# Linear attention followed by two expert stages: TensorE work of the attention grouped by tile shape, state in two buffers, state product in the rotating banks, powers of w in PSUM

## The chip, the cores and the metric

One core of one Trainium2 chip. The metric is the device time of one execution in microseconds (us), the median of several runs of the same program. Engines by the profile's names: PE (TensorE) and PEld (its weight loads), DVE (VectorE), ACT (ScalarE), POOL (GpSimd), SP (the queue that issues most DMAs). Each engine works through its own list of instructions in order; between engines there are semaphores.

## The reference

Three stages; the change touches only the first. All of it is fp32.

```
def _attn_ref(r, k, v, w, u):               # r, k, v: (4, 8, 768, 48)
    for t in range(S):
        cur = einsum('bhd,bhe->bhde', u * k[t], v[t])
        y[t] = einsum('bhd,bhde->bhe', r[t], state + cur)
        state = w * state + einsum('bhd,bhe->bhde', k[t], v[t])
x = attn_out as (3072, 384)
x = top-1 of 8 experts, softmax gate, relu(x @ w1[e]) @ w2[e]
out = g(x @ w_in) @ w_out,  g(h) = h - tanh(h)
```

## The kernel before

The 768 tokens of each of the 4 batches are cut into 6 chunks of 128. A step n is one chunk of one batch: `seq = [(c, b) ...]`, chunks outer, batches inner, so 24 steps (NN = 24) and a last half step that only finishes. The 8 heads lie as 4 pairs j with a half q each: partitions 64q to 64q+47 hold head 2j+q, and the pad up to 64 is zero. Per step:

- `load(n)` (L230) brings r, k, v by token (`n_b`, 576 KB) and r, k by dimension (`t_b`, two transfers of 192 KB), five buffers each, issued by SP three steps ahead. `w_load` (L66) brings 384 KB of the first expert's weights in every second step up to n = 15; `w_split` (L79) cuts them into a rounded part (ACT, L84) and a rest (DVE, L85).
- POOL makes `rk` (L317), `rku` (L323) and `kh` (L332), 128x384 each, two steps ahead, and `sw` (L376), the decayed state.
- DVE sums `rku` over each head into `dt` (`diag_sum`, L337), multiplies `t` by the powers of w in PRK (`scale`, L312, 1024 columns), and copies the scores below the diagonal into `am` (`mask`, L359, one instruction per half). `am` comes from ACT, eight diagonal tiles per step (`diag`, L344).
- PE makes the scores A (`scores`, L353, 64-row tiles), the state product Pp (`state`, L370, tiles of 48 columns), the output from the state (`outp`, L393, full 128x128 tiles against Sb, a block-diagonal copy of the state) and the output within the chunk (L398, 48 columns), and transposes finished outputs of seven steps ago (`xout`, L524). fp32 matmuls show as two instructions each.
- ACT copies the output Yp to SBUF (L403), the state into the block diagonal (`state_copy`, L385) and the transposed rows to `xs` (L531), which go to DRAM.
- Once in four steps the chunk just finished is gated: `logits` (L413, at n mod 4 = 1), `logits2` and `gate` (n mod 4 = 2, on PE, DVE, ACT), `rank_mm` and `rank_sel` (n mod 4 = 3: DVE up to `lo` and `ol`, then `hv` L490 and `rh` on POOL), `idx_mm` (n mod 4 = 0).

The order of each engine's list is the order of the calls in the loop at L702 (`manual_schedule`); nothing reorders it. PSUM has eight banks: yh0 and yh1 hold Yp, yh2 holds Pp, A0 and A1 the scores, sm the small products, and two banks with the tag X are taken in turn by Xps, lps and others: the third taker waits for the readers of the first.

```
        st["S", b] = n                  # end of state(n): Sc[b] = sw + Pp, in place
        ...
            if 1 <= n <= NN:
                outp(n - 1)             # L712, before scores(n)
                if n > 1:
                    state_copy(n - 1)
```

Of the kernel before, what the change touches and what calls it, by code (L numbers as in the profile page):

```python
# [8 lines left out]
F32 = mybir.dt.float32  # L9
# [6 lines left out]
ALU = mybir.AluOpType  # L16
# [14 lines left out]
def rwkv_moe_moe_kernel(ctx: ExitStack, tc: tile.TileContext, rk_t, rkv, pk, u, wp1, wp2, out):  # L31
# [141 lines left out]
    def bc(ap, shape):  # L173
        return ap.to_broadcast(shape)
# [27 lines left out]
    Sc = [ap_.tile([P, HP, D], F32, name=f"Sc{b}") for b in range(B)]  # L202
    Sb = [ap_.tile([P, HP, P], F32, name=f"Sb{b}") for b in range(B)]
# [3 lines left out]
    PRK = ap_.tile([P, 2, HP, P], F32, name="PRK")  # L207
# [5 lines left out]
    yh = [psy.tile([P, BANK], F32, tag=f"y{d}", name=f"yh{d}")[:, 0:HEAD] for d in range(KD)]  # L213
    Yp = [t.rearrange("p (j t) -> p j t", t=P) for t in yh[0:2]]
    Pb = yh[2]
    Pp = Pb[:, 0:HP * D].rearrange("p (j d) -> p j d", d=D)
# [52 lines left out]
    def tables():  # L269

        for t, base, n in ((pw, wsafe.unsqueeze(2), 16), (pq, pw[:, :, 16:17], 8)):
            nc.vector.memset(t[:, :, 0:1], 1.0)
            nc.vector.tensor_copy(out=t[:, :, 1:2], in_=base)
            m = 1
            while m < n:
                nc.vector.tensor_tensor(out=t[:, :, m + 1:2 * m + 1], in0=t[:, :, 1:m + 1],
                                        in1=bc(t[:, :, m:m + 1], [P, HP, m]), op=ALU.mult)
                m *= 2
        table(nc.gpsimd, PRK[:, 0], pq[:, :, 0:8], pw[:, :, 0:16])
        nc.vector.reciprocal(out=ipw, in_=pw)  # L280
        nc.vector.reciprocal(out=ipq, in_=pq)
        nc.vector.tensor_tensor(out=ipl, in0=ipq, in1=bc(pq[:, :, 8:9], [P, HP, 9]), op=ALU.mult)
        table(nc.vector, PRK[:, 1], ipq[:, :, 0:8], ipw[:, :, 1:17])

# [78 lines left out]
    def state(n):  # L363
        c, b = seq[n]
        if c == C - 1:
            return
        kh = st.pop(("kh", n))
        for j in range(HP):
            for q in range(2):
                nc.tensor.matmul(Pp[64 * q:64 * q + D, j, :], lhsT=kh[:, 2 * j + q, :],  # L370
                                 rhs=n_b[n % NB][:, 2, 2 * j + q, :], start=True, stop=True)
        if c == 0:
            nc.vector.tensor_copy(out=Sc[b], in_=Pp)
        else:
            sw = at2.tile([P, HP, D], F32, tag="sw", name="sw")
            nc.gpsimd.tensor_tensor(out=sw, in0=Sc[b], in1=bc(pq[:, :, 8:9], [P, HP, D]), op=ALU.mult)  # L376
            nc.vector.tensor_tensor(out=Sc[b], in0=sw, in1=Pp, op=ALU.add)
        st["S", b] = n

    def state_copy(n):  # L380
        c, b = seq[n]
        if c == C - 1:
            return
        for q in range(2):
            nc.scalar.copy(out=Sb[b][64 * q:64 * q + 64, :, 64 * q:64 * q + D], in_=Sc[b][64 * q:64 * q + 64, :, :])  # L385

    def outp(n):
        c, b = seq[n]
        am = st.pop(("am", n))
        for j0 in range(0, HP, 2):  # L390
            for j in (j0, j0 + 1):
                if c > 0:
                    nc.tensor.matmul(Yp[j % 2][:, j // 2, :], lhsT=Sb[b][:, j, :], rhs=t_b[n % NB][:, 0, j, :],  # L393
                                     start=True, stop=False)
            for j in (j0, j0 + 1):
                for q in range(2):
                    p0 = 64 * q
                    nc.tensor.matmul(Yp[j % 2][p0:p0 + D, j // 2, :], lhsT=n_b[n % NB][:, 2, 2 * j + q, :],  # L398
                                     rhs=am[:, q, j, :], start=(c == 0), stop=True)
        if b == 0:  # L400
            st["y", c] = yp.tile([P, HP, B, P], F32, tag="y", name="y")
        for i in range(2):
            nc.scalar.copy(out=st["y", c].rearrange("p (j i) b t -> p i j b t", i=2)[:, i, :, b, :], in_=Yp[i])  # L403

    sm = ps1.tile([P, 512], F32, tag="sm", name="sm")
# [203 lines left out]
    def by_token():  # L609

        with tc.tile_pool(name="slow", bufs=1) as sp:
# [3 lines left out]
            for b in range(B):  # L615
                nc.vector.memset(Sc[b], 0.0)
# [5 lines left out]
            for c in range(C):  # L622
                st["y", c] = yp.tile([P, HP, B, P], F32, tag="y", name="y")
                for b in range(B):
# [5 lines left out]
                    with tc.For_i(0, P, 1) as t:  # L630
# [8 lines left out]
                        nc.vector.tensor_add(out=cur, in0=cur, in1=Sc[b])  # L639
# [7 lines left out]
                        nc.vector.tensor_tensor(out=Sc[b], in0=Sc[b], in1=bc(wcol.unsqueeze(2), [P, HP, D]), op=ALU.mult)  # L647
                        nc.vector.tensor_add(out=Sc[b], in0=Sc[b], in1=kv)
# [12 lines left out]
    with tc.manual_schedule():  # L661
        w_cols()
        identity()
        for i in range(2):
# [8 lines left out]
        zero_states()  # L673
# [23 lines left out]
        for t in Yp + [Pp]:  # L697
            nc.vector.memset(t, 0.0)
# [3 lines left out]
        for n in range(NN + 1):  # L702
            if n + 3 < NN:
                load(n + 3)
            if n % 2 == 1 and n // 4 < PRE:
                w_load(n // 4, n // 2 % 2)
            if n + 1 < NN:
                diag_sum(n + 1)
                scale(n + 1)
            at_step(n, 2, logits)  # L710
            if 1 <= n <= NN:
                outp(n - 1)  # L712
                if n > 1:
                    state_copy(n - 1)
            for m in XOUT.get(n, (n - LAG,)):
                if m >= 0:
                    xout(m)
            if 0 < n < NN - 1:
                diag(n + 1)
            if n < NN:  # L720
                scores(n)
                mask(n)
                if n == 0:
                    k_table()
                    diag(1)
                else:
                    if n == 1:
                        state(0)
                    state(n)
            if n == 1:  # L730
                state_copy(0)
            if n + 2 < NN:
                side(n + 2)
                if n == 0:
                    side_kh(0)
                    side_kh(1)
                side_kh(n + 2)
# [8 lines left out]
            if n < NN:  # L746
                at_step(n, 5, idx_mm)
            if n == NN - 2:
                head_gather()
# [651 lines left out]
```

## Time and profile before

| what | us |
|---|---|
| median of 3 runs | 825.17 (825.07 to 829.99) |
| the profiled execution | 828.9 |
| its span, first to last instruction | 826.8 |
| PE busy | 786.1 (95%) |
| DVE busy | 649.6 (79%) |
| ACT busy | 526.5 (64%) |
| POOL busy | 448.3 (54%) |

The profiled execution is one run; its time is the span and 2.1 us around it. Times in rows count from the start of the span. Busy shares are means over all three stages; the attention is the stretch up to about 154 us, after which the expert stages follow on the same core.

### The profile page before, as it was taken

To read this page: it belongs to the slowest core of one execution; us is meant where nothing else is said; L and a number is where in the kernel's file an instruction comes from. 1 tells how busy PE (TensorE), PEld (TensorE's weight loads), DVE (VectorE), ACT (ScalarE), POOL (GpSimd) and SP (SyncE) were. 2 spreads that over 40 slices of the span, in tenths; PEclk is the share of its full clock that TensorE was granted. 3 is DMA by queue.
4 is the path that set the end of the run, shared out by engine and by line. 5 is a ranking of instruction groups with operands and counts; after the bars stand their busy time and mean duration, and the time that the engine had idled before them with its cause. 6 is when DMAs were issued, how large, how long until landed. Compare 5 with 4: busy or idle time off the path is not lost.

```text
span 826.8 us, 14401 instructions
## 1 busy us (share of the span) xinstructions
PE 786.1 (95%) x5052; PEld 702.3 (85%) x5052; DVE 649.6 (79%) x1127; ACT 526.5 (64%) x1135; POOL 448.3 (54%) x438
## 2 busy tenths in 40 slices
PE   7799999989999999997999999999999999999995
PEld 6576766789888999996989999999999999999895
DVE  6789888548888888876469888888888888888991
ACT  7778887515454444443478776776777677677870
POOL 5977876226675886656525535335344344443533
PEclk9799999999999999999999999999999999999999
DMA  8988774226688989897410000000000000000000
GB/s 202 246 222 238 220 211 129 99 71 201 201 227 236 256 224 267 258 250 177 110 56 2 1 1 39 1 1 39 1 1 29 10 1 17 23 1 0 39 1 38
DMA packets 34979, 89.88 MB, mean 109 GB/s; under 512 B 5690, under 2 KB 13022, under 8 KB 34896
## 3 DMA queue, kind: packets, MB, share of 16 engines
q1 hardware_dynamic: 30704, 78.87, 34.5%
q0 software_dynamic: 4192, 9.99, 3.9%
q8 instruction: 42, 0.69, 0.4%
q14 instruction: 41, 0.34, 0.2%
HBM read 73.10 MB, written 15.74 MB: 107 GB/s over the span
## 4 chain that ended last, share of the span: by engine, by line
PE 48%; DVE 2%; issue 1%; POOL 1%; ACT 0%; POOLq 0%; DVEq 0%; ACTq 0%
PE h L1237 23%; PE o L1285 22%; PE y L1011 2%; PE hps L986 1%; DVE t L1258 0%; DVE h L1255 0%; DVE h L1256 0%; DVE h L1254 0%; DVE t L1253 0%; POOL out_dram L1298 0%; POOL g L1274 0%; ACT g L1273 0%; POOLq L1396 0%; ACT z L1241 0%; ACT t L1243 0%
## 5 line engine op out<-in xcount | busy, mean ns | idle before, releaser
L1237 PE MATMUL h<-xb,ring 128*128 128x512 f32 x864 | 215.9, 395 | 0.7 <-DVE t L1258 0.7
L1274 POOL TENSOR_TENSOR g<-t,g 128x512 fp32r<-128x512 f32 x93 | 120.5, 1295 | 176.3 <-ACT g L1273 121.3
L1285 PE MATMUL o<-ring,g 128*128 128x384 f32 x1116 | 209.3, 336 | 0.0
L1285 PEld LDWEIGHTS o<-ring,g 128*128 128x128 f32 x1116 | 196.1, 188 | 8.1
L1237 PEld LDWEIGHTS h<-xb,ring 128*128 128x128 f32 x864 | 161.3, 188 | 31.9 <-DVE t L1258 1.1
L85 POOL TENSOR_TENSOR ring<-stg,ring 128x384 fp32r<-128x384 f32 x102 | 104.9, 1057 | 39.6 <-ACT ring L84 23.9
L1241 ACT ACTIVATE z<-h 128x512 f32<-128x512 f32 x96 | 57.5, 599 | 97.9 <-PE h L1237 97.8
L1011 PE MATMUL y<-h,ring 128*128 128x256 f32 (+7 forms) x576 | 115.5, 345 | 0.0
L986 PE MATMUL hps<-xt,ring 128*128 128x472 f32 (+6 forms) x504 | 106.8, 355 | 8.4 <-DVE xt L975 4.1
L1011 PEld LDWEIGHTS y<-h,ring 128*128 128x128 f32 x576 | 102.6, 190 | 3.5 <-DVE h L990 0.4
L986 PEld LDWEIGHTS hps<-xt,ring 128*128 128x128 f32 x504 | 90.7, 188 | 13.7 <-DVE xt L975 5.5
L1253 DVE TENSOR_TENSOR t<-t,h 128x512 f32<-128x512 f32 x96 | 65.8, 686 | 43.0 <-ACT t L1243 42.9
L84 ACT CAST ring<-stg 128x384 fp32r<-128x384 f32 x152 | 71.1, 511 | 29.3 <-DMA stg<-in_wp_dram 24.9
L1258 DVE COPY_PREDICATED t<-mk,h 128x512 f32<-128x512 uint32 x96 | 72.2, 752 | 9.9
L1255 DVE SCALAR_TENSOR_TENSOR h<-s,h 128x512 f32<-128x512 f32 x96 | 66.9, 696 | 10.0
L1245 ACT ACTIVATE s<-z,gb 128x512 f32<-128x512 f32 x96 | 69.6, 725 | 0.0
L1256 DVE SCALAR_TENSOR_TENSOR h<-z,h 128x512 f32<-128x512 f32 x96 | 66.8, 695 | 3.3
L1247 ACT ACTIVATE mk<-z,gt 128x512 f32<-128x512 f32 x96 | 69.3, 722 | 0.0
L989 ACT ACTIVATE h<-hps 128x256 fp32r<-128x256 f32 (+7 forms) x64 | 32.0, 501 | 57.7 <-PE hps L986 55.3
L1254 DVE TENSOR_TENSOR h<-h,z 128x512 f32<-128x512 f32 x96 | 66.5, 693 | 0.0
L344 ACT ACTIVATE am<-ident,dt 128x128 f32<-128x128 f32 x192 | 58.6, 389 | 7.0 <-DVE dt L337 6.9
L1273 ACT CAST g<-t 128x512 fp32r<-128x512 f32 x93 | 57.6, 619 | 8.0 <-DVE t L1258 5.8
(233 smaller groups left out, 1116.2 us busy)
## 6 DMA issues: line engine op xcount, KB each, us to landing
stg<-in_wp_dram SPq DMA_DIRECT2D x64, 384.0 KB
n<-in_rkv_dram SPq DMA_DIRECT2D x24, 576.0 KB
d<-in_wp_dram SPq DMA_DIRECT2D x32, 384.0 KB
t<-in_rk_t_dram SPq DMA_DIRECT2D x48, 192.0 KB
wdec<-dcf SPq DMA_DIRECT2D x32, 192.0 KB
xd<-xs SPq DMA_DIRECT2D x24, 192.0 KB
stg<-wdec SPq DMA_DIRECT2D x12, 384.0 KB
wl<-wdec SPq DMA_DIRECT2D x2, 768.0 KB
```

What stands on the lines that cost most here:

```text
L84: nc.scalar.copy(out=dst[:, 0, sl], in_=of)
L85: eng.tensor_tensor(out=dst[:, 1, sl], in0=of, in1=dst[:, 0, sl].bitcast(F32), op=ALU.subtract)
L986: nc.tensor.matmul(ps, lhsT=wf(a, kk), rhs=xt[e][b][:, kk, :], start=(n == 0), stop=(n == 8))
L1011: nc.tensor.matmul(yps[d], lhsT=wf(a)[:, d * P:(d + 1) * P], rhs=h2[:, b, :], start=(f == 0 and n == 0), stop=(f == CH1 - 1 and n == 2))
L1237: nc.tensor.matmul(ps, lhsT=wf(a, kk), rhs=xb[j][:, b, kk, :], start=(n == 0), stop=(n == 8))
L1245: nc.scalar.activation(out=s, in_=z, func=ACTF.Square, scale=G_K ** 0.5, bias=gb)
L1247: nc.scalar.activation(out=mk, in_=z, func=ACTF.Relu, scale=-1.0, bias=gt2)
L1255: nc.vector.scalar_tensor_tensor(out=ps, in0=s, scalar=G_K * G_D, in1=ps, op0=ALU.add, op1=ALU.mult)
L1256: nc.vector.scalar_tensor_tensor(out=ps, in0=z, scalar=G_A, in1=ps, op0=ALU.subtract, op1=ALU.mult)
L1258: nc.vector.copy_predicated(out=t, mask=mk.bitcast(U32), data=ps)
L1274: nc.gpsimd.tensor_tensor(out=g[:, 1, :], in0=ww, in1=g[:, 0, :].bitcast(F32), op=ALU.subtract)
L1285: nc.tensor.matmul(ops[q], lhsT=gg[i][:, b, q * P:(q + 1) * P], rhs=wf(a), start=(f == 0 and n == 0), stop=(f == CH2 - 1 and n == 2))
```

## The change

1. `outp` no longer uses the block-diagonal Sb: the output from the state is 8 matmuls with lhsT of 64 rows and 48 columns straight from the state `Sc`, which now has two buffers per batch (chunk parity). All 8 come first, then all 8 within the chunk, into one bank Yp. `state_copy` and `zero_states` go. So that rows 48 to 63 of the state are zero, `kh` gets 64 columns (three fixed buffers, pads zeroed once) and the state product writes 64 rows.
2. The state product Pp takes one of the two X banks instead of yh2. The powers of w (PR, PK) lie in the banks yh1 and yh2 that this leaves free, both made by DVE; `scale` becomes two instructions of 512 columns.
3. `y_copy` is one copy of 512 columns, called two steps later.
4. The order within a step: scores, mask, scale(n+1), xout, logits2 and gate, rank, idx, logits, state, output of step n-1, and POOL's side work last. Before: scale(n+1), logits, output of n-1, state copy, xout, diag, scores, mask, state, side work, logits2 and gate, rank, idx.

```diff
-        table(nc.gpsimd, PRK[:, 0], pq[:, :, 0:8], pw[:, :, 0:16])
+        table(nc.vector, PR, pq[:, :, 0:8], pw[:, :, 0:16])
...
-        nc.vector.tensor_tensor(out=t, in0=t, in1=PRK, op=ALU.mult)
+        for i, pw_ in enumerate((PR, PK)):
+            nc.vector.tensor_tensor(out=t[:, i], in0=t[:, i], in1=pw_, op=ALU.mult)
...
+        Pp = ps1.tile([P, HP, P], F32, tag="X", name="Pp", bufs=2)[:, :, 0:D]
...
-                nc.tensor.matmul(Pp[64 * q:64 * q + D, j, :], lhsT=kh[:, 2 * j + q, :],
+                nc.tensor.matmul(Pp[64 * q:64 * q + 64, j, :], lhsT=kh[:, 2 * j + q, :],
...
-                    nc.tensor.matmul(Yp[j % 2][:, j // 2, :], lhsT=Sb[b][:, j, :], rhs=t_b[n % NB][:, 0, j, :],
-                                     start=True, stop=False)
...
+                    nc.tensor.matmul(Yp[p0:p0 + D, j, :], lhsT=Sc[b][(c - 1) % 2][p0:p0 + 64, j, :],
+                                     rhs=t_b[n % NB][p0:p0 + 64, 0, j, :], start=(j == 0), stop=False)
...
             if n + 1 < NN:
                 diag_sum(n + 1)
-                scale(n + 1)
-            at_step(n, 2, logits)
-            if 1 <= n <= NN:
-                outp(n - 1)
...
+            at_step(n, 2, logits)
+            if 0 < n < NN:
+                if n == 1:
+                    state(0)
+                state(n)
+            if n > 0:
+                outp(n - 1)
```

POOL's list around step 15, before: `hv` and `rh` of the rank stand behind the side work of step 15 (the first `sw`, `rk`, `rku`, `kh` here).

```order
L376 TENSOR_TENSOR sw<-Sc_143,pq 128x192 [waits DVE_49]
L317 TENSOR_TENSOR rk<-n_132 128x384 [waits DMAHW4_49]
L323 TENSOR_TENSOR rku<-rk,ub 128x384 [waits DVE_49,Pool_49]
L332 TENSOR_TENSOR kh<-n_132,KT 128x384 [waits PE_49]
L490 TENSOR_TENSOR hv<-OH,ohh 128x128 [waits DVE_49,Activation_49]
L494 TENSOR_TENSOR rh<-hv,tileid 128x4x32 [waits Pool_49]
```

The same four and the same pair in the changed kernel:

```order
L487 TENSOR_TENSOR hv<-OH,ohh 128x128 [waits DVE_49,Activation_49]
L491 TENSOR_TENSOR rh<-hv,tileid 128x4x32 [waits Pool_49]
L376 TENSOR_TENSOR sw<-Sc_146,pq 128x192
L315 TENSOR_TENSOR rk<-n_132 128x384 [waits DMAHW4_49]
L321 TENSOR_TENSOR rku<-rk,ub 128x384 [waits Pool_49]
L330 TENSOR_TENSOR kh_158<-n_132,KT 128x8x48 [waits PE_49]
```

`hv` has moved ahead of the `sw` of step 15 and of the `rk` and `rku` of step 17; what it waits for on DVE is the same.

PE's list in step 17 (the one with the logits), before: logits, then the two halves of the output, the transposes, the scores, and the state product into its own bank yh_159.

```order
L413 MATMUL lps<-y,wgp 32x512 [waits Activation_49] x2
L413 MATMUL lps<-y,wgp 32x512 x2
L393 MATMUL yh_157<-t_126,Sb_144 128x128
...
L524 MATMUL Xps<-ident,y 128x128 x3
L353 MATMUL A_1706<-t_127 128x128 [waits DMAHW5_49,PE_49]
...
L370 MATMUL yh_159<-n_132,kh 48x48 [waits DMAHW4_49,DVE_49]
```

The same step in the changed kernel, from the transposes on; the row of Pp is the first state matmul, yh_159 is now Yp, L387 is the output from the state and L392 the output within the chunk.

```order
L521 MATMUL Xps<-ident,y 128x128 [waits Activation_49]
L521 MATMUL Xps<-ident,y 128x128 x3
L410 MATMUL lps<-y,wgp 32x512 [waits DVE_49,Activation_49]
L410 MATMUL lps<-y,wgp 32x512 x3
L369 MATMUL Pp<-n_132,kh_158 64x48 [waits DMAHW4_49,Activation_49,Pool_49]
L369 MATMUL Pp<-n_132,kh_158 64x48 x7
L387 MATMUL yh_159<-t_126,Sc_141 48x128 x8
L392 MATMUL yh_159<-am,n_131 48x128 x8
L351 MATMUL A_1768<-t_128 128x128 [waits DMAHW1_49,DVE_49]
```

The output now stands behind the state product, and the state product waits for ACT: in this step Xps and lps have taken both X banks, so Pp takes the bank of Xps of the same step, whose reader is `xs`.

## Rows read from the trace of the kernel before

**Rows 1.** Windows: busy of PE, PEld, DVE, ACT, POOL (count), PEclk, DMA share, GB/s.

```profile
30.00:40.00 10.00, 7.30 (x92) 5.94 (x86) 6.68 (x11) 6.95 (x23) 9.77 (x10) 0.72 1.02 247
100.00:120.00 20.00, 18.18 (x229) 13.12 (x223) 16.82 (x35) 15.29 (x47) 14.45 (x16) 1.00 0.78 219
```

**Rows 2.** Timeline of PE, scores of steps 4 and 20: start, length, instruction.

```profile
37.37 2.08 PE L353 MATMUL A<-t 64*128 64x128 f32 x16
...
132.77 1.16 PE L353 MATMUL A<-t 64*128 64x128 f32 x16
```

**Rows 3.** Timeline of PE, step 13, from its scores to its last transposes.

```profile
91.49 1.16 PE L353 MATMUL A<-t 64*128 64x128 f32 x16
92.58 0.56 PE L370 MATMUL yh<-n,kh 128*48 128x48 f32 x16
93.08 0.71 PE L393 MATMUL yh<-t,Sb 128*128 128x128 f32 x4
93.72 1.01 PE L398 MATMUL yh<-am,n 128*48 128x128 f32 x8
...
95.30 0.65 PE L398 MATMUL yh<-am,n 128*48 128x128 f32 x8
95.88 0.66 PE L524 MATMUL Xps<-ident,y 128*128 128x128 f32 x4
```

**Rows 4.** Timeline of DVE, steps 15 and 16, and the gate of step 22.

```profile
103.38 0.54 DVE L337 TENSOR_REDUCE dt<-rku 128x8 f32<-128x384 f32 x1
103.85 1.21 DVE L312 TENSOR_TENSOR t<-t,PRK 128x1024 f32<-128x1024 f32 x1
104.98 1.32 DVE L359 COPY_PREDICATED am<-mlt,A 128x512 f32<-128x512 uint32 x2
106.20 0.34 DVE L377 TENSOR_TENSOR Sc<-sw,yh 128x192 f32<-128x192 f32 x1
106.45 0.18 DVE L476 TENSOR_TENSOR pr<-sm,OH 128x32 f32<-128x32 f32 x1
...
107.59 0.69 DVE L501 TENSOR_TENSOR ol<-iotaf,lo 128x512 f16<-128x512 f32 x1
...
110.35 1.56 DVE L312 TENSOR_TENSOR t<-t,PRK 128x1024 f32<-128x1024 f32 x1
...
146.16 0.18 DVE L428 TENSOR_REDUCE m<-sm 128x4 f32<-128x32 f32 x1
...
147.85 0.16 DVE L451 TENSOR_TENSOR cums<-cum,bump 128x8 f16<-128x8 f16 x1
```

**Rows 5.** Timeline of POOL, side work and rank of steps 14 to 16.

```profile
99.43 1.00 POOL L317 TENSOR_TENSOR rk<-n 128x384 f32<-128x384 f32 x1
100.51 1.00 POOL L323 TENSOR_TENSOR rku<-rk,ub 128x384 f32<-128x384 f32 x1
...
107.63 0.92 POOL L490 TENSOR_TENSOR hv<-OH,ohh 128x128 f16<-128x128 f16 x1 [5.16 <-DVE lo L488]
...
109.45 1.38 POOL L317 TENSOR_TENSOR rk<-n 128x384 f32<-128x384 f32 x1
110.91 1.87 POOL L323 TENSOR_TENSOR rku<-rk,ub 128x384 f32<-128x384 f32 x1
```

**Rows 6.** Timeline of ACT, step 16: transposed rows, then the diagonals.

```profile
110.55 0.58 ACT L531 ACTIVATE xs<-Xps,gt 128x384 f32<-128x384 f32 x1
111.03 2.44 ACT L344 ACTIVATE am<-ident,dt 128x128 f32<-128x128 f32 x8
```

**Rows 7.** One line's instructions: DVE with one operand in PSUM (min/median/max ns).

```profile
L1253 DVE TENSOR_TENSOR t<-t,h x96: 657/688/691, 418.7 to 805.0; 128x512 f32<-128x512 f32 x96
```

**Rows 8.** Timeline around step 3: DVE's sum and PE's output.

```profile
32.19 0.55 DVE L337 TENSOR_REDUCE dt<-rku 128x8 f32<-128x384 f32 x1 [2.51 <-POOL rku L323]
...
34.98 2.46 PE L398 MATMUL yh<-am,n 128*48 128x128 f32 x16 [2.70 <-DVE am L359]
```

**Rows 9.** Timeline of PE at the end: scores of step 23, first work after the attention.

```profile
149.12 1.16 PE L353 MATMUL A<-t 64*128 64x128 f32 x16
...
153.49 0.88 PE L564 MATMUL hp<-ident,n 128*128 128x128 f32 x6
```

More of the change, by code (lines that the diff above doesn't have):

```diff
@@ L212, in rwkv_moe_moe_kernel @@
     KT = ap_.tile([P, H, D], F32, name="KT")
[L213 to L216, printed above, removed]
+    kh_b = [ap_.tile([P, H, 64], F32, name=f"kh{i}") for i in range(3)]
+    yb = [psy.tile([P, BANK], F32, tag=f"y{d}", name=f"yh{d}") for d in range(KD)]
+    yh = [t[:, 0:HEAD] for t in yb]
+    Yp, PR, PK = (t.rearrange("p (j t) -> p j t", t=P) for t in yb)
     headn = ap_.tile([P, 1], F32, name="headn")
@@ L367, in state @@
         kh = st.pop(("kh", n))
+        Pp = ps1.tile([P, HP, P], F32, tag="X", name="Pp", bufs=2)[:, :, 0:D]
         for j in range(HP):
             for q in range(2):
-                nc.tensor.matmul(Pp[64 * q:64 * q + D, j, :], lhsT=kh[:, 2 * j + q, :],
+                nc.tensor.matmul(Pp[64 * q:64 * q + 64, j, :], lhsT=kh[:, 2 * j + q, :],
                                  rhs=n_b[n % NB][:, 2, 2 * j + q, :], start=True, stop=True)
+        new = Sc[b][c % 2]
         if c == 0:
-            nc.vector.tensor_copy(out=Sc[b], in_=Pp)
+            nc.vector.tensor_copy(out=new, in_=Pp)
         else:
             sw = at2.tile([P, HP, D], F32, tag="sw", name="sw")
[L376 to L385, printed above, removed]
+            nc.gpsimd.tensor_tensor(out=sw, in0=Sc[b][(c - 1) % 2], in1=bc(pq[:, :, 8:9], [P, HP, D]), op=ALU.mult)
+            nc.vector.tensor_tensor(out=new, in0=sw, in1=Pp, op=ALU.add)
     def outp(n):
@@ L389, in outp, with y_copy @@
         am = st.pop(("am", n))
-        for j0 in range(0, HP, 2):
-            for j in (j0, j0 + 1):
-                if c > 0:
-                    nc.tensor.matmul(Yp[j % 2][:, j // 2, :], lhsT=Sb[b][:, j, :], rhs=t_b[n % NB][:, 0, j, :],
-                                     start=True, stop=False)
-            for j in (j0, j0 + 1):
+        if c > 0:
+            for j in range(HP):
                 for q in range(2):
                     p0 = 64 * q
-                    nc.tensor.matmul(Yp[j % 2][p0:p0 + D, j // 2, :], lhsT=n_b[n % NB][:, 2, 2 * j + q, :],
-                                     rhs=am[:, q, j, :], start=(c == 0), stop=True)
+                    nc.tensor.matmul(Yp[p0:p0 + D, j, :], lhsT=Sc[b][(c - 1) % 2][p0:p0 + 64, j, :],
+                                     rhs=t_b[n % NB][p0:p0 + 64, 0, j, :], start=(j == 0), stop=False)
+        for j in range(HP):
+            for q in range(2):
+                p0 = 64 * q
+                nc.tensor.matmul(Yp[p0:p0 + D, j, :], lhsT=n_b[n % NB][:, 2, 2 * j + q, :],
+                                 rhs=am[:, q, j, :], start=(c == 0 and j == 0), stop=(j == HP - 1))
+    sm = ps1.tile([P, 512], F32, tag="sm", name="sm")
+    def y_copy(n):
+        c, b = seq[n]
         if b == 0:
             st["y", c] = yp.tile([P, HP, B, P], F32, tag="y", name="y")
-        for i in range(2):
-            nc.scalar.copy(out=st["y", c].rearrange("p (j i) b t -> p i j b t", i=2)[:, i, :, b, :], in_=Yp[i])
-    sm = ps1.tile([P, 512], F32, tag="sm", name="sm")
+        nc.scalar.copy(out=st["y", c][:, :, b, :], in_=Yp)
     idx_ps = sm[:, 0:E * 4]
@@ L663, in rwkv_moe_moe_kernel @@
         identity()
+        for t in kh_b:
+            nc.gpsimd.memset(t[:, :, D:], 0.0)
         for i in range(2):
@@ L696, in rwkv_moe_moe_kernel @@
         side(1)
-        for t in Yp + [Pp]:
-            nc.vector.memset(t, 0.0)
+        nc.vector.memset(Yp, 0.0)
         nc.gpsimd.memset(cum[0], 0.0)
@@ L725, in rwkv_moe_moe_kernel @@
                     diag(1)
[L726 to L737, printed above, removed]
+            if n + 1 < NN:
+                scale(n + 1)
+            for m in XOUT.get(n, (n - LAG,)):
+                if m >= 0:
+                    xout(m)
             at_step(n, 3, logits2)
@@ L747, in rwkv_moe_moe_kernel @@
                 at_step(n, 5, idx_mm)
+            at_step(n, 2, logits)
[3 more added lines that the diff above has]
+                state(n)
+            if n > 0:
+                outp(n - 1)
+            if n == NN:
+                y_copy(NN - 1)
+            if n + 2 < NN:
+                side(n + 2)
+                if n == 0:
+                    side_kh(0)
+                    side_kh(1)
+                side_kh(n + 2)
             if n == NN - 2:
```

32 lines of the change are left out of this document (11 added, 21 removed).

## The prediction

> **What bounds the kernel now.** I read the windows first. Of the stretch 30 to 40 us PE is busy for 7.3 of 10 us at a granted clock of 0.72, while the DMA engines are full (share 1.02, 247 GB/s); from 100 to 120 us the clock is 1.00, the DMA share 0.78, and PE and DVE are busy for 18.2 and 16.8 of 20 us [rows 1]. So the early steps share a transfer limit, and the later ones are held by PE and DVE together. The pace is read from the scores of steps 4 and 20: 132.77 - 37.37 = 95.4 us for 16 steps, or 23.85 us for each cycle of four (the gating work comes once in four) [rows 2].
>
> Within a step, PE is back to back: in step 13 the scores take 92.58 - 91.49 = 1.09 us, the state product 0.50, the first half of the output from the state 0.64, the transposes 0.58, eight matmul instructions of the output within the chunk 0.58 [rows 3]. DVE goes from one instruction to the next as well: sum 0.47, scale 1.13, mask 1.22, state add 0.25, rank 1.14 up to ol [rows 4]. A step that is shorter on one engine alone gains only until the other is late.
>
> **What the change does, part by part.**
>
> Output on PE. Now: two halves, each 0.64 + 0.58 us, so 2.44 us [rows 3]. New: 16 instructions of 64x48 tiles, then 16 of 128x48. No row shows 64x48 tiles. The nearest is the scores: 16 instructions of 64x128 tiles, q by q in turn as here, in 1.09 us; and 16 within the chunk are one group with one start, about 2 x 0.58 - 0.15 = 1.0 us [rows 3]. I take 1.03 + 1.0, so 0.4 us less per step. Bounds for the 64x48 part: 0.5 us at the low end (the state product's 16 narrow instructions), 16 x 0.64/4 = 2.6 us at the high end, if they run one by one like full tiles; I take the row that it is nearest to. State product with 64 instead of 48 columns: 0.50 to 0.58. PE then needs 1.09 + 0.58 (transposes) + 0.58 + 1.03 + 1.0 = 4.28 us per step.
>
> A rule speaks against this part. The Trainium skill, TensorEngine Tiling (Array Packing), Gotcha 1, says that different row tiles cannot access one PSUM bank at the same time. The scores of before put their two row tiles into A0 and A1; the new output puts both into Yp, in different partitions. No row of before shows two row tiles in one bank. By the rule the sum is that of the third rival, by the row of the scores the one below.
>
> Scale on DVE. The trace has this form: one operand in SBUF, one in PSUM, 512 columns, 688 ns [rows 7]; two in a row take some 1.30 us, 1.20 to the next start (the two masks: 1.32 and 1.22 [rows 4]). The old one takes 1.21 us alone and 1.56 when POOL works, and POOL's rku then takes 1.87 instead of 1.00 [rows 4, 5]. So the gain is some 0.3 us per step on DVE and up to 0.9 on POOL, where both met; at worst 0.1 is lost.
>
> ACT. The two state copies and one of the output copies go, over 1 us per step. ACT is not late in the plain steps, and I give this nothing by itself; if it were, the gain would be hidden in the same cycle below.
>
> The new order. mask(n) no longer waits behind scale(n+1), and PE no longer waits for the mask of the step before, since the output comes a step later in its list. That takes away the early wait of 2.70 us [rows 8]. But two waits are added, and these I price.
>
> First, POOL's hv of the rank now stands ahead of sw(n), rk(n+2) and rku(n+2). hv waits for DVE's lo, which ends as ol begins; from there hv, rh and sw take 109.45 - 107.59 = 1.86 us, rk 1.08 and rku 1.00 [rows 4, 5]: 3.94 us until DVE can start the sum for step n+2. Queued behind that sum are mask(n+1), scale(n+2) and so the scores of n+2. In the old order POOL stood idle for 5.16 us before hv with this work already done [rows 5].
>
> Second, in the step with the logits the state product takes the bank of that step's Xps and waits for xs. On ACT, xs stands behind the eight diagonals (2.44 us), which wait for the sum. Queued behind the state product on PE are the whole output and the next scores; for those DVE waits.
>
> The new cycle, followed from mask(14) to mask(18), with starts from [rows 3 to 6] and small ends estimated from them:
> - step 14: mask 1.22, scale 1.20, gate 147.85 + 0.16 - 146.16 = 1.85, add 0.25, split 0.5, sum 0.47: 5.5 us.
> - step 15: mask 1.22, scale 1.20, rank 1.14: 3.6 us.
> - POOL until the sum can start: 3.9 us.
> - step 16: sum 0.47, mask 1.22, scale 1.20, index sum 0.2, add 0.25, split 0.5, sum 0.47: 4.3 us.
> - step 17: diagonals 2.4, xs 0.58, state 0.58, output 1.03 + 1.0, scores 1.16: 6.75 us.
>
> That is 24.05 us. The split still has both operands in SBUF and meets POOL twice on this path; the rows show up to 0.87 us for such a meeting (1.87 against 1.00), and I take half of both, 0.9: 24.95, or 1.1 us more than the 23.85 of now. The gain per step is real, but the two waits give it back.
>
> The sum, against the profiled execution (828.9 us: span 826.8 and 2.1 around it):
> - Up to the scores of step 4: POOL's sum for step 4 ends about 1 us earlier without the meetings, scale (1.5) no longer stands between the sum and mask(3) but comes after it, and the scores of step 4 no longer stand behind the output of step 3 (2.46 us from 34.98 [rows 8]). With the sum at 31.2, mask to 32.9, scale to 34.2, the scores start at 34.3 instead of 37.37 [rows 2]: -3.1. Bounds: 0, if the transfers hold the side work, and -4.
> - Steps 4 to 7, where the rank comes first at 7: a step's transfers are 960 KB and half a w_load of 384 KB, 1.18 MB, 4.8 us at 247 GB/s [rows 1]; four steps 19.1 and the first rank wait 1.9, so 21.0 instead of 23.85: -2.9. Bounds: 0 and -4.
> - Steps 8 to 19, three cycles: +3.3. Bounds below, with the rivals.
> - Steps 20 to 23 come out even: the rank wait of step 19 falls here, and plain steps are shorter.
> - The end: 153.49 - 149.12 = 4.37 us from the last scores to the next stage [rows 9]. New: scores 1.09, two sets of transposes 1.16, rank 0.4, output of step 22 2.03, its copy out of the single bank 0.6, output of step 23 2.03: 7.3. +2.9.
>
> Together +0.2 us: nothing that a measurement of this kernel tells from no change (about 1%, 8.25 us). The profiled execution stood 3.7 us above the median of the runs; against the median of 825.17 the forecast is 825.4 us. The cover of this sum is the first expert stage, which follows PE and moves with the end of the attention.
>
> **Rivals.**
>
> The waits don't come about. If POOL keeps so far ahead that rku is ready in spite of hv, and xs comes early, PE's own work sets the cycle: 4 x 4.28 + logits 1.0, second logits 0.9, rank 0.4, index 0.3 = 19.7 us (the small ones estimated from their place in the list); with hand-offs 21. Then three cycles give -8.6 instead of +3.3, and the sum is -11.7: 813.5 us; at 20 a cycle, 810.5. For it: in both engines' sums (DVE's is 18.4) there is room, and POOL idles 5 us a cycle. Against it: the lists of POOL and PE, which fix these waits; POOL idles because it waits for lo, and cannot run past it.
>
> TensorE's clock falls in the new waits. In each cycle PE would stand still twice for 2 us or more, in steps 16 and 17. After the 2.70 us before 34.98 the same 16 instructions took 2.46 us instead of about 1.1, and the next scores 2.08 instead of 1.16 [rows 2, 3, 8], in a stretch at a granted clock of 0.72 [rows 1], between the levels of 1.2 and 2.4 GHz. On the path behind the second wait stand state, output and scores, 3.8 us; at half speed they cost up to 3 us more per cycle. It decides if the scores behind the second wait take 2 us. Sum: 0.2 + 3 x 3 = +9.2, 834.4 us, slower than before. For it: the early rows. Against it: around these waits PE is still busy for four fifths of the cycle, more than in 30 to 40 us.
>
> The row tiles block each other in the one bank. Then the output from the state costs up to 2.6 us instead of 1.03. PE's cycle is 19.7 + 4 x 1.6 = 26.1 us at worst; by the step-17 leg alone it is 24.95 + 1.6 = 26.5. With half of that excess the sum is 0.2 + 3 x 0.8, and 1 in the steps before and 0.8 at the end: +4.4, 829.6 us; with all of it 834 us, slower than before. The rule that speaks for it is the one cited above from the Trainium skill. Against it: the column tiles of the old output share a bank and take 0.58 us for eight.
>
> **How the numbers follow.** Waits as priced, no change: 0.51. Waits absent, faster: 0.24. Clock: 0.16, mostly over 1% slower. Row tiles: 0.07, half of it over 1%. The rest, 0.02, on either side. Of the likeliest case's own range, 818 to 832, nothing lies beyond 1%. Faster by over 1% (below 816.9): 0.24 from the first rival, with its ends beyond the line kept there: 0.23. Slower (above 833.4): 0.13 from the clock, 0.04 from the tiles, and 0.03 from larger waits than mine: 0.20. Within 1%: 0.57. The range of eight in ten reaches into both sides, 811 to 837.
>
> **What would show it.** In the changed kernel's profile: no meeting of scale and POOL (two scales of 0.69, rku at 1.00); the output from the state 1.0 us per step; POOL's hv followed by sw and rk with DVE's sum waiting for POOL rku by 1 us or more in steps 12, 16 and 20; PE waiting for ACT xs before the state product in steps 9, 13 and 17; the scores of step 4 near 34 us; cycles of 25 us. Cycles of 21 us, or no such waits, would prove the sum wrong on the fast side; rows of 2 us for the scores behind the waits, with a granted clock well under 1, on the slow side; a 64x48 group of 2 us would be the third rival.

## The result and the profile after

The changed kernel takes 832.2 us (median of 5 runs, 828.8 to 833.73) against 826.27 us for the kernel before in the same comparison: ratio 1.0064, 95% interval 1.0035 to 1.0093. Forecast were 825.4 us, 811 to 837, and most likely no change that this measurement can tell (57%). The time lies in the range and the change is under 1%, but it is a small loss, not zero. Later groups of runs were on other chips, where the kernel before takes 821 to 822 us; so ratios are compared, not times. In one of these groups the changed kernel came to 1.0091 (1.0055 to 1.0127).

The windows that answer to [rows 1], and as a third row the second half of the second stretch:

```profile
30.00:40.00 10.00, 7.65 (x84) 5.84 (x78) 8.98 (x19) 8.13 (x26) 8.87 (x10) 0.69 1.01 268
100.00:120.00 20.00, 14.87 (x215) 11.74 (x213) 13.28 (x29) 11.57 (x34) 15.80 (x18) 0.91 0.60 193
110.00:120.00 10.00, 7.30 (x80) 5.49 (x82) 5.58 (x12) 5.56 (x16) 9.11 (x10) 0.83 0.44 139
```

From 100 to 120 us PE was busy for 18.2 of 20 us at a clock of 1.00; now it is 14.9 at 0.91, and DVE went from 16.8 to 13.3. Neither engine is full any more: the steps are held by waits. PE's timeline, steps 4, 13, 14 and 17, answers to [rows 2, 3]:

```profile
32.67 1.27 PE L351 MATMUL A<-t 64*128 64x128 f32 x16 [2.07 <-issue]
...
85.20 2.17 PE L351 MATMUL A<-t 64*128 64x128 f32 x16 [2.19 <-issue]
...
90.46 0.67 PE L369 MATMUL Pp<-n,kh 128*64 128x48 f32 x16 [1.06 <-POOL kh L330]
91.06 1.08 PE L387 MATMUL yh<-t,Sc 64*48 64x128 f32 x16
...
93.08 1.16 PE L351 MATMUL A<-t 64*128 64x128 f32 x16
...
110.27 1.25 PE L351 MATMUL A<-t 64*128 64x128 f32 x16 [2.19 <-issue]
...
115.53 1.00 PE L369 MATMUL Pp<-n,kh 128*64 128x48 f32 x16 [2.43 <-POOL kh L330]
116.46 1.95 PE L387 MATMUL yh<-t,Sc 64*48 64x128 f32 x16
...
119.70 1.16 PE L351 MATMUL A<-t 64*128 64x128 f32 x16
```

The output from the state takes 1.08 us, 1.01 to the next start, as forecast. Both new waits stand there: 2.19 us before the scores of steps 13 and 17, and 1.06 and 2.43 us before the state product. The profile names no releaser for the first; the scale that these scores read ends at 110.17 (below), 0.1 us before the scores of step 17. The last wait is put down to POOL's `kh`, but that had long been done; ACT's `xs` ends at 115.43 (below), 0.1 us before Pp starts. Such a label names one of several semaphores; here the ends of the instructions tell which one was late. After the 2.43 us the same work runs slow: 1.95 us where step 13 has 1.08. The granted clock from 110 to 120 us is 0.83, that is, part of the stretch at 1.2 GHz and part at 2.4. The price can be read: from its scores to its state product each of the two steps takes 5.26 us, and from there to the next scores step 13 takes 2.62 us (90.46 to 93.08) and step 17 takes 4.17 (115.53 to 119.70), so the slow clock costs 1.55 us.

DVE, steps 15 and 16 (answers to [rows 4]), and POOL (answers to [rows 5]):

```profile
102.85 0.15 DVE L485 SCALAR_TENSOR_TENSOR lo<-hs,RK 128x4 f32<-128x4 f32 x1
...
104.98 0.35 DVE L377 TENSOR_TENSOR Sc<-sw,Pp 128x192 f32<-128x192 f32 x1 [1.24 <-POOL sw L376]
...
107.20 0.55 DVE L335 TENSOR_REDUCE dt<-rku 128x8 f32<-128x384 f32 x1 [0.89 <-POOL rku L321]
107.67 1.33 DVE L357 COPY_PREDICATED am<-mlt,A 128x512 f32<-128x512 uint32 x2
108.89 1.28 DVE L310 TENSOR_TENSOR t<-t,yh 128x512 f32<-128x512 f32 x2
```

```profile
103.08 0.92 POOL L487 TENSOR_TENSOR hv<-OH,ohh 128x128 f16<-128x128 f16 x1 [9.07 <-DVE lo L485]
104.07 0.40 POOL L491 TENSOR_TENSOR rh<-hv,tileid 128x128 f16<-128x128 f16 x1
104.43 0.52 POOL L376 TENSOR_TENSOR sw<-Sc,pq 128x192 f32<-128x192 f32 x1
104.90 1.00 POOL L315 TENSOR_TENSOR rk<-n 128x384 f32<-128x384 f32 x1
105.98 1.19 POOL L321 TENSOR_TENSOR rku<-rk,ub 128x384 f32<-128x384 f32 x1
```

POOL stands for 9.07 us in front of `hv` (5.16 before), and its `sw`, `rk` and `rku` behind it make DVE wait twice: 1.24 and 0.89 us. From the end of `lo` to the start of the sum pass 4.20 us; forecast were 3.94. The two scales take 1.28 us together, where the old one took 1.56 beside POOL. ACT in step 17 (answers to [rows 6]), and PE at the end (answers to [rows 9]):

```profile
112.52 2.45 ACT L342 ACTIVATE am<-ident,dt 128x128 f32<-128x128 f32 x8 [0.93 <-DVE dt L335]
114.87 0.56 ACT L528 ACTIVATE xs<-Xps,gt 128x384 f32<-128x384 f32 x1
```

```profile
136.69 2.17 PE L351 MATMUL A<-t 64*128 64x128 f32 x16 [3.04 <-issue]
138.79 1.97 PE L521 MATMUL Xps<-ident,y 128*128 128x128 f32 x8
141.03 1.94 PE L410 MATMUL lps<-y,wgp 128*32 128x512 f32 x8 [0.28 <-ACT xs L528]
142.90 1.11 PE L387 MATMUL yh<-t,Sc 64*48 64x128 f32 x16
...
149.04 1.16 PE L351 MATMUL A<-t 64*128 64x128 f32 x16
...
156.28 0.87 PE L561 MATMUL hp<-ident,n 128*128 128x128 f32 x6
```

The attention ends 2.8 us later than before (156.28 against 153.49, the first `hp`). One more difference lies behind it, in POOL's first gather for the expert stage; first the kernel before, then the changed one:

```profile
177.75 0.95 POOL L962 DMA_INDIRECT xg<-xd,idx  x1 [7.67 <-PE hp L591]
```

```profile
186.47 0.94 POOL L961 DMA_INDIRECT xg<-xd,idx  x1 [13.74 <-DVE tok L867]
```

It starts 24.3 us behind hp before the change, and 30.2 after it, waiting for another engine.

### The profile page after: what moved, and what is told of

Read it like the earlier page. It is cut to its first block, busy times and chain, and to the rows that moved or that the text cites. A ratio compares the mean times of both kernels' runs of the same rounds, so it can differ in the third digit from the quotient of the medians.

```text
span 831.6 us, 14663 instructions
## 1 busy us (share of the span) xinstructions
PE 780.8 (94%) x5212; PEld 704.2 (85%) x5212; DVE 648.6 (78%) x1150; ACT 508.7 (61%) x1067; POOL 430.2 (52%) x440
## 4 chain that ended last, share of the span: by engine, by line
PE 47%; DVE 2%; issue 1%; POOL 1%; ACT 0%; POOLq 0%; DVEq 0%; ACTq 0%
PE h L1236 23%; PE o L1284 22%; PE y L1010 1%; PE hps L985 1%; DVE t L1257 0%; DVE h L1254 0%; DVE h L1255 0%; DVE h L1253 0%; DVE t L1252 0%; POOL out_dram L1297 0%; POOL g L1273 0%; ACT g L1272 0%; POOLq L1395 0%; ACT z L1240 0%; ACT t L1242 0%
## 5 line engine op out<-in xcount | busy, mean ns | idle before, releaser
L84 ACT CAST ring<-stg 128x384 fp32r<-128x384 f32 x152 | 71.0, 512 | 20.0 <-DMA stg<-in_wp_dram 18.5
```

Of the source, the lines that this page charges most:

```text
L84: nc.scalar.copy(out=dst[:, 0, sl], in_=of)
```

## The experiments

The twelve runs, by their profiles; "cycle" is from the scores of step 10 to those of step 14, of 14 to 18, and of 18 to 22. The cycles of a row are those of one profiled execution, and two such profiles of the changed kernel differ by 1.6 us in the first cycle:

| kernel | cycles, us | first hp at | gather behind hp | ratio to before (95%) |
|---|---|---|---|---|
| before (rows shown) | 23.8, 24.1, 23.1 | 153.5 | 24.3 | 1 |
| before again (e9) | 23.8, 23.6, 23.1 | 149.9 | 24.1 | 1 |
| changed | 24.8, 26.6, 25.2 | 156.3 | 30.2 | 1.0064 (1.0035 to 1.0093) |
| changed again (e5) | 26.4, 26.4, 24.6 | 156.4 | 31.2 | 1.0091 (1.0055 to 1.0127) |
| e1, POOL's side work first | 26.4, 23.4, 23.2 | 153.6 | 31.4 | 1.0075 (1.0025 to 1.0126) |
| e2, logits last | 24.7, 24.4, 26.1 | 153.2 | 30.4 | 1.0100 (1.0073 to 1.0127) |
| e3, both | 23.6, 24.2, 22.9 | 148.7 | 31.1 | 1.0010 (0.9985 to 1.0035) |
| e4, gap in SBUF | 25.1, 26.6, 24.4 | 156.5 | 25.1 | 1.0064 (1.0044 to 1.0083) |
| e6, matmuls in the waits | 27.1, 27.4, 27.4 | 165.6 | 30.1 | 1.0261 (1.0217 to 1.0306) |
| e7, both, scale two ahead | 23.9, 25.1, 21.9 | 150.2 | 30.5 | 1.0023 (0.9998 to 1.0048) |
| e8, that with gap, split, index | 22.5, 22.0, 21.6 | 142.3 | 24.3 | 0.9898 (0.9874 to 0.9922) |
| e10, e8 with scale one ahead | 20.3, 20.3, 21.5 | 137.5 | 24.1 | 0.9833 (0.9797 to 0.9868) |
| e11, e8 with powers in SBUF | 22.5, 22.9, 23.1 | 148.8 | 24.4 | 0.9986 (0.9961 to 1.0011) |
| e12, e11 with logits in yh2 | 23.0, 23.7, 21.8 | 147.8 | 25.4 | 0.9977 (0.9956 to 0.9999) |

### The two waits, one at a time and together

e1 puts the POOL part of the rank behind the step's side work:

```diff
                 side_kh(n + 2)
+            at_step(n, 4, rank_pool)    # hv and rh, taken out of rank_sel
```

> The changed kernel with one edit: hv and rh of the rank (POOL, and rh's second half on ACT) are called after the side work of the step instead of ahead of it, as before the change. Theory W (the two waits that the new lists add set the cycle): DVE no longer waits for POOL rku in the steps with n mod 4 = 0; these shrink from 7.2-7.9 us to about 5.5, the cycle from scores 10 to scores 14 from 24.81 to about 22.8; three to four cycles give -6 to -9 us against the changed kernel's 832.2: 823 to 826. The step with the logits (n mod 4 = 1) keeps its wait for xs. Rival theory L (the load of PE or DVE sets the cycle, and a wait taken away comes back elsewhere): cycle 24.5 to 25, time 830 to 833. Rival theory C (the falls of TensorE's clock are the whole loss): the cycles with the clock at 1.00 stay at 24.8, only the disturbed ones come to that: -4, about 828.

e2 calls the logits behind the output:

```diff
-            at_step(n, 2, logits)
             if 0 < n < NN:
...
                 outp(n - 1)
+            at_step(n, 2, logits)
```

> The changed kernel with one edit: logits is called behind the output of the step, so that the state product takes the X bank that the logits took and no longer the bank of the same step's Xps. Theory W: no wait of the state product for xs; the steps with n mod 4 = 1 shrink from 7.9 (9.4 in step 17) to about 5.5 to 6, the cycle 10 to 14 from 24.81 to about 22.5; the clock fall in step 17, which followed that wait, goes as well; -7 to -10 us: 822 to 825. Theory L: cycle 24.5 to 25, 830 to 833. Theory C: only steps 17 and 21 get shorter, -4: about 828.

e3 has both edits:

> Both edits together. Theory W: the first rival of the prediction comes true, PE's own work sets the cycle, 20 to 21.5 us (a small wait of the index product for rh, up to 1 us in four steps, is in that), clock 1.00 from 60 us on; 15 to 18 us less than the changed kernel: 814 to 817, faster than the kernel before by over 1%. Theory L: 824 or more. Theory C: about 828.

Measured, e1: DVE's waits for POOL's `rku` and `sw` are gone, and steps 12 and 16 fall from 7.2 and 7.5 us to 6.0 and 6.2. But the state product still waits up to 2.4 us for `xs`, and behind that wait the clock falls in step 13 (9.26 us, and 26.4 for the cycle; the two cycles without a fall take 23.4 and 23.2). e2: Pp no longer waits for `xs`, and step 17 falls from 9.43 to 5.95 us. Yet its first cycle is 24.7: step 12 grew to 7.9 us, since the wait for POOL is still there and a new wait took the place of the one removed. DVE's list of waits in e2 shows it:

```profile
DVE ring L85 <- ACT ring L84: 10.4, 6, 3.2
DVE dt L335 <- POOL rku L321: 4.3, 4, 1.7
```

ACT's half of the weight split stands behind the copy of the logits in ACT's list. With the logits called late, that copy is late, then the split on ACT, then the split on DVE (up to 3.2 us of waiting; 0.7 in the changed kernel), and behind it the sum, the mask and the scale. e3 shortens the attention by 7.6 us and reaches the kernel before in time; its cycle of 23.6 is far from the 20 to 21.5 that theory W wanted, and the same wait for ACT's half of the split stands in it. DVE in e3, step 13 (the split, and the sum and the mask behind it), and ACT there:

```profile
91.49 0.94 DVE L85 TENSOR_TENSOR ring<-stg,ring 128x384 fp32r<-128x384 f32 x1 [2.22 <-ACT ring L84]
92.35 0.54 DVE L335 TENSOR_REDUCE dt<-rku 128x8 f32<-128x384 f32 x1
92.82 1.34 DVE L357 COPY_PREDICATED am<-mlt,A 128x512 f32<-128x512 uint32 x2
```

```profile
90.46 0.59 ACT L413 COPY lt<-lps 128x512 f32<-128x512 f32 x1 [0.91 <-PE lps L410]
90.94 0.52 ACT L84 CAST ring<-stg 128x384 fp32r<-128x384 f32 x1
```

So theory W held for each wait by itself, and failed in the sum: two waits removed left a third, made by one of the edits.

### The loss behind the attention

e4 adds one unused tile, so that the pools behind it lie where they lay before:

```diff
     idf = ap_.tile([P, E * 4], F32, name="idf")
+    gap = ap_.tile([P, 1920], F32, name="gap")
```

> The changed kernel with an unused SBUF tile of 7,680 bytes per partition in the attention's pool, so that the pools behind it lie where they lay before. Theory M (the loss of 1.9 us behind the attention comes from the memory layout: the buffer of the first gathered expert rows now lies over a buffer of the gating pool and waits for DVE's tok): the first xg gather starts 24 us behind the first hp transposes, as before (24.3), not 30.2; from hp to the end 673.3 to 673.9 us instead of 675.3; time 830 to 830.8. Rival theory N (the 1.9 us are the spread of the transfers in the first expert stage): the gather may move, the end doesn't: 832.

The gather moves as theory M says: 25.1 us behind hp. In all profiles of the table it starts 24.1 to 25.4 us behind hp where the pools lie as before, and 30.1 to 31.4 where they don't. In the built program one of the four buffers of the gathered rows lies over `lt`, a tile of the gating pool, in the changed kernel; before, and with the gap, none does. In the time nothing is seen: the ratio is 1.0064, as without the gap. What the late gather costs is to be read on PE, from its first `hps` matmul in this stage to the first that reads `xt`; first the kernel before, then the changed one:

```profile
184.31 3.50 PE L986 MATMUL hps<-ring,ring 128*128 128x256 f32 x27 [0.57 <-DVE ring L584]
...
200.69 1.66 PE L986 MATMUL hps<-xt,ring 128*128 128x472 f32 x7
```

```profile
186.30 3.49 PE L985 MATMUL hps<-ring,ring 128*128 128x256 f32 x27
...
205.14 1.66 PE L985 MATMUL hps<-xt,ring 128*128 128x472 f32 x7
```

The stretch takes 16.4 us before and 18.8 after. It takes 16.4 us in all seven profiles where the pools lie as before, e4 among them, and 17.4 to 20.3 in the seven where they don't; in the second profile of the changed kernel it takes 17.9. So the late gather costs the changed kernel 1.5 to 2.5 us, 0.2 to 0.3% of the whole, less than these ratios can tell. For the rest of that stage one more profile of each kernel was taken:

> The changed kernel once more, unaltered, so that its profile comes from the same chip as those of this group: steps 10 to 14 in 24.8 us as before; about 1.006 of the kernel before. Its stretch from hp to the end is the measure for the runs beside it, since that stretch differs from chip to chip.

> The kernel before, unaltered, for a profile from the chip of this group: scores of step 4 to step 20 in 95.4 us as in the rows shown, hp at 153.5. Its stretch from hp to the end shows how much of the changed kernel's loss lies behind the attention: 669 us or more, and the loss there is the gather's 1.5 us alone (theory M); 666 or less, and another 3 us are lost there (theory N2, the transfers).

From hp to the end the kernel before takes 673.3 and 673.6 us, the changed one 675.3 and 669.9, e4 667.7. The 673.6 is above the 669 of the expectation, so no further 3 us are lost there; but these profiles come from different chips, and between two profiles of the changed kernel lie 5.4 us, more than the 1.9 that were to be explained. So the gather's move and its price at the start of the stage are shown, and a further loss there is not.

### The clock

e6 puts matmuls without use where PE waits:

```diff
+            if n % 4 == 1 and n > 4:
+                warm_sm(12)             # then scores(n)
...
             at_step(n, 2, logits)
+            if n % 4 == 1 and n > 4:
+                warm_sm(8)              # then state(n)
```

> The changed kernel with 12 matmuls of 128x128 without use ahead of the scores of steps 9, 13, 17 and 21, and 8 ahead of the state product of the same steps, where PE waits: PE stands less, and everything else is as it was. Theory C (the falls of the clock in steps 17, 20 and 21 add time of their own): the granted clock stays at 1.00 from 100 to 150 us, step 17 comes from 9.43 to about 7.9 us, step 21 from 8.25 to about 7.9; 2 to 4 us less than the changed kernel. Theory W (the waits alone make the length, the clock falls within their slack): all steps as long as before, or longer by what the useless matmuls overrun, 0 to +3 us.

The first part missed its aim. The twelve write into the bank that the index sum of DVE reads, and so waited for it (2.24 us) and ran only after the wait: 2.94 us of extra work in each such step. The scores came later by that, and ACT's diagonals did not: in step 17 `xs` ended at 122.03, before the logits were through, so the eight had hardly a wait left to fill and took 2 us more. All cycles became longer. What the run does show is the price of the clock. The granted clock is 1.00 in every window of 10 us from 60 to 150 us, and from the state product to the next scores step 17 takes 2.62 us, as step 13 does in the changed kernel, where step 17 takes 4.17:

```profile
124.27 0.67 PE L369 MATMUL Pp<-n,kh 128*64 128x48 f32 x16
...
126.89 1.16 PE L351 MATMUL A<-t 64*128 64x128 f32 x16
```

So the fall in step 17 is worth 1.55 us. (The whole step, 7.28 us in place of 9.43, can't be compared, since its waits differ.) In step 21 the changed kernel takes 6.21 us from the scores to the output (136.69 to 142.90), and e6 takes 3.46 up to its useless matmuls (146.80 to 150.26): another 2.7 us. Waits of 2.24 and 3.08 us stand in e6 as well, right ahead of the twelve, and no fall follows them; so a wait of that length alone doesn't bring the fall, and no run here shows what does. What the kernel would take without the falls isn't shown either.

### What set the cycle then

e7 takes e3 and scales two steps ahead:

```diff
-            if n + 1 < NN:
+            if n < 7:
                 scale(n + 1)
+            if 6 <= n and n + 2 < NN:
+                scale(n + 2)
```

> Both edits of the third run, and from step 6 on scale(n+2) in place of scale(n+1) in step n. With both edits the cycle fell to 23.6 us only, not to 20 or 21. Theory D (what is left is the hand-off on DVE: the scores of step n+1 wait for a scale that stands behind the mask of step n, the split and the gate): a scale two steps ahead takes the wait of the scores away, and the cycle comes to 20.5 to 22; 5 to 9 us less than with both edits. Theory L (DVE's own load, 17.7 us and its meetings with POOL, sets the cycle): 23 to 24, no gain.

e8 is e7 with the gap of e4 and two calls moved; the split goes ahead of the logits, the index product behind the output:

```diff
                 outp(n - 1)
+            if n >= 3 and (n - 3) // 4 < PRE:
+                w_split((n - 3) // 4, (n - 3) % 4)
             at_step(n, 2, logits)
+            if n < NN:
+                at_step(n, 5, idx_mm)
```

> As the run before, with the unused SBUF tile of the fourth run, the split of the weights ahead of logits (so that its ACT half doesn't stand behind the copy of the logits), and the index product behind the output. Theory D with W and M: cycle 20 to 21.5; the first gather 24 us behind hp; 10 us or more less than the kernel before, ratio 0.985 to 0.99. If the first expert stage is held by its transfers, part of that is given back behind the attention: ratio 0.993 to 0.998.

> The best kernel so far (ratio 0.990) with scale(n+1) in place of scale(n+2). Theory D (the hand-off over scale held PE once the other waits were gone): cycle back from 22.5 to about 23.5, 3 to 4 us slower. Theory S (the split in ACT's and DVE's lists was what held the cycle, and the earlier scale is worth nothing, as between the two runs before it): within 1 us of the best kernel.

e7 brings nothing over e3 (1.0023 against 1.0010): theory D fell. e8 brings 1.0% over the kernel before; against e7 its attention ends 8.0 us earlier, and the gap gives 2.1 us at the start of the expert stage (16.4 us in place of 18.5). Which of the two moved calls brings the 8.0 us wasn't tried apart; DVE's longest wait for ACT's half of the split falls from 2.5 us in e3 to 0.8. e10 has the same calls without the earlier scale and is better still, 0.9833; so the earlier scale was no help but a loss, against both theories of that run. Its cycles of 20.3 us are what the first rival of the prediction gave for PE's own work with hand-offs (19.7, and 21). PE in e10, steps 12 and 13:

```profile
73.73 1.16 PE L352 MATMUL A<-t 64*128 64x128 f32 x16
74.82 0.66 PE L526 MATMUL Xps<-ident,y 128*128 128x128 f32 x4
75.41 0.67 PE L370 MATMUL Pp<-n,kh 128*64 128x48 f32 x16
76.01 1.08 PE L388 MATMUL yh<-t,Sc 64*48 64x128 f32 x16
77.02 1.08 PE L393 MATMUL yh<-am,n 128*48 128x128 f32 x16
78.03 0.36 PE L512 MATMUL sm<-rh,ol 128*128 128x32 f16 x8
78.60 1.34 PE L352 MATMUL A<-t 64*128 64x128 f32 x16 [0.21 <-PE sm L512]
...
83.33 1.06 PE L411 MATMUL lps<-y,wgp 128*32 128x512 f32 x8 [0.18 <-DVE Sc L378]
84.33 1.16 PE L352 MATMUL A<-t 64*128 64x128 f32 x16
```

PE goes from one group to the next, and no wait of this stretch is over 0.3 us. Why the earlier scale costs time isn't settled. In e8 the logits wait 1.93 us for `xs` in step 13, and its splits on DVE take 876 ns on average where those of e10 take 663, which points to more meetings with POOL; that a scale one step earlier brings these meetings about was only argued.

### The powers of w in PSUM, alone

e11 is e8 with the powers in SBUF and one scale of 1024 columns (the unused tile is smaller by as much, so the pools behind it lie as in e8); e12 also gives the logits the bank yh2 that this frees.

```diff
-        for i, pw_ in enumerate((PR, PK)):
-            nc.vector.tensor_tensor(out=t[:, i], in0=t[:, i], in1=pw_, op=ALU.mult)
+        nc.vector.tensor_tensor(out=t, in0=t, in1=PRK, op=ALU.mult)
```

> The best kernel with the powers of w in SBUF again, and scale as one instruction of 1024 columns. By the prediction's term (0.3 us per step on DVE, up to 0.9 us on POOL at each meeting): scale 1.21 to 1.56 in place of 1.26, POOL's rku up to 1.9 where both meet, 1 to 4 us slower than the best kernel. Rival: the powers in PSUM bring nothing, within 1 us.

```diff
-        ps = ps1.tile([P, B * P], F32, tag="X", name="lps", bufs=2)
+        ps = yb[2]
```

> As the run before, and the logits in the bank yh2 that the powers leave free, so that nothing in the step with the logits waits for xs. In the best kernel the logits wait 1.93 us for xs in step 13. Theory B (the bank is worth more to the logits than to the powers): steps with n mod 4 = 1 from 7.3 to about 5.5, 4 to 7 us less than the run before, ahead of the best kernel. Theory A (ACT or DVE is late next): less than 2 us.

e11 against e8: 0.9986 against 0.9898, about 7 us; hp comes 6.5 us later. The groups of lines from 55 to 135 us show where, POOL's `kh` and the scale, first e8, then e11:

```profile
L311 DVE TENSOR_TENSOR t<-t,yh 128x512 f32<-128x512 f32 x28 | 17.8, 674 | 0.0
L331 POOL TENSOR_TENSOR kh<-n,KT 128x384 f32<-128x384 f32 x14 | 15.0, 1071 | 0.0
```

```profile
L332 POOL TENSOR_TENSOR kh<-n,KT 128x384 f32<-128x384 f32 x14 | 23.6, 1685 | 0.0
L312 DVE TENSOR_TENSOR t<-t,PRK 128x1024 f32<-128x1024 f32 x15 | 21.3, 1422 | 0.0
```

With both operands in SBUF the scale meets `kh`, which takes 1685 ns instead of 1071; a scale takes 1422 ns on average instead of about 1260 for a pair of halves. The Trainium skill, SBUF — State Buffer, SBUF: two separate sides, says that a DVE operation with two inputs in SBUF and a POOL operation that reads SBUF exclude each other for the whole instruction. The rows agree: with one input in PSUM the stretching of `kh` nearly goes. Some 3.7 of the 6.5 us fall in one step, that before the scores of step 8, where e8 and e11 both make two scales in a row (2.60 and 3.69 us) and the gate follows; so part of this gain hangs on that edit. And not all of it is the meetings themselves: PE's clock falls in e11 (granted clock 0.83 from 50 to 60 us and from 100 to 110, 0.87 from 130 to 140) and not in e8 (1.00 from 30 us on). In step 7 of e11 the work from the state product to the next scores takes 3.89 us, and 2.62 in e8 (49.75 to 52.37):

```profile
52.98 0.67 PE L371 MATMUL Pp<-n,kh 128*64 128x48 f32 x16 [1.77 <-DVE Sc L379]
...
56.87 1.46 PE L353 MATMUL A<-t 64*128 64x128 f32 x16
```

With steps 16 and 20, where the output takes 3.64 and 3.16 us in place of 2.02, the slow clock makes some 4 of the 6.5 us. e12 brings 0.1% over e11, within the intervals: nothing in its step 13 waits for `xs` any more (5.3 us in place of 6.8), but steps 11 and 12 grew (6.1 and 6.4 us, from 4.6 and 6.0), and the state product now waits up to 1.4 us for DVE: theory A.

## Why the prediction was right, and where it was wrong

Each term of the sum, against the two profiles of each kernel (the rows shown and the changed kernel's first; e9 and e5):

| term | forecast | first pair | second pair |
|---|---|---|---|
| up to the scores of step 4 | -3.1 | -4.7 | -2.5 |
| steps 4 to 7 | -2.9 | -3.7 | -3.8 |
| steps 8 to 19 | +3.3 | +5.1 | +7.5 |
| steps 20 to 23 | 0 | +3.3 | +2.3 |
| the end | +2.9 | +2.9 | +2.9 |
| behind hp | 0 | +1.9 | -3.6 |
| sum | +0.2 | +4.7 | +2.8 |

- **The two added waits** were right in place and size: POOL's path 4.2 us for 3.94, the state product held by `xs` behind the diagonals, and 24.81 us for a cycle for which 24.95 was forecast. By legs, from mask(14) to mask(18) on DVE, the changed kernel takes 5.2, 3.5, 4.2, 5.3 and 8.4 us, where 5.5, 3.6, 3.9, 4.3 and 6.75 were forecast and 0.9 for the split; of the last, 1.55 is the clock. The sum's own wait for `rku` in step 16 is 0.89 us and not over 1, as the sign had it, since 1.24 us of the delay stand ahead of it, at `sw`. e1 and e2 take one wait each away, and the row it stood in goes; each alone leaves the time as it is, and both together bring it to that of the kernel before (1.0010).
- **"Steps 20 to 23 come out even"** failed. The rank wait of step 19 does fall there, as was said, but I set plain steps against it that PE did not get: the scores of step 21 wait 3.04 us, and then 6.2 us of work at half clock or nearly so follow, 2.7 of them the price of the clock. So most of this term is the second rival as well, which I had priced behind the wait for `xs` only.
- **Steps 8 to 19** were mis-sized by 1.8 us, and that is the second rival, the clock, in one cycle of three (26.62 for 24.81). I gave it 16% and wrote that PE is still busy for four fifths of the cycle; the windows show 0.83 and 0.81 where it happens. In the second profile it happens in two cycles. In steps 9 and 13 of the first the clock falls too (0.83 from 60 to 70 and from 80 to 90 us), but ahead of the state product, while that waits for `xs`, and there it costs nothing: from scores to state product these steps take 5.32 and 5.26 us, and step 17 5.26. The price did not reach 3 us in each cycle, so the loss stayed under 1%.
- **The sum** came within 4.5 us in part by luck. Up to the scores of step 8 the first pair is 2.4 us better than forecast, and behind them 6.9 us worse; some 4.3 us of that, in steps 17 and 21, are the clock, to which the sum gave nothing. Two profiles of one kernel differ by up to 2.8 us in the first term (the scores of step 4 at 37.4 and 34.6 before) and by 5.4 in the last, so these two can't be sized better than that.
- **"The cover of this sum is the first expert stage, which follows PE"** was not quite true: smaller tiles moved the pools, and the gather of that stage waits for other readers. The order of instructions could not show it, since it is in the addresses; its price is 1.5 to 2.5 us.
- **The row tiles in one bank** don't block each other. The Trainium skill, TensorEngine Tiling (Array Packing), Gotcha 1, says that different row tiles cannot access one PSUM bank at the same time; here 16 instructions of two row tiles into the one bank take 1.08 us, and the scores, into two banks, 1.16. The measurement decides, and this rival is out.
- **The first rival** (waits absent, 810.5 to 813.5) was wrong for this change and right as a bound: e10, with the lists put in order, reaches 20.3 us a cycle and 0.983 of the time before, some 14 us. The change had the gain in it, and its own order gave it back.
- **The powers in PSUM** I priced at 0.3 us per step on DVE and then at nothing, as hidden. In e8 they are worth some 7 us (e11): `kh` on POOL is stretched, not `rku` (1.07 us in e11, 1.02 in e8), and some 4 of the 6.5 us on the attention are the slow clock. With the order of e10, without the two scales in a row, it wasn't tried.

## What to carry to other kernels

When a change reorders several engines' lists, price every in-order list that it touches, also the ones that only follow: here the gain came only with three lists put right at once (POOL's rank, PE's bank, ACT's split; the index product was moved along with it), and each of the first two repairs alone showed nothing in the time, because the next list was late. Where a rotating bank gets a third taker, look at who reads the bank before it, and on which engine that reader stands behind other work. A tile taken out of SBUF moves all that is allocated behind it, and so the waits of a later stage: compare what the first transfers of that stage wait for.

## What was not expected of the hardware

- The clock fell after waits of 2 to 3 us in the midst of a stretch at 1.00 (110 to 120 us: 0.83; the same output in 1.95 us for 1.08), though not after each of them: the wait of 2.19 us before the scores of step 17 was followed by scores of 1.25 us, the same wait before those of step 13 by 2.17, and waits of 2.24 and 3.08 us in e6 by work at full speed. Where the work behind it waited for another engine anyway, a fall cost nothing (steps 9 and 13); in step 17 it cost 1.55 us.
- Meetings of DVE and POOL stretched `kh` from 1.07 to 1.69 us on average, from 55 to 135 us, and one operand of the scale in PSUM did away with most of it.
